# Eleven upper halves taken straight from the gate's PSUM bank, with a new order of work, in a fused attention and gated feed-forward kernel

## The chip, the cores and the metric

The kernel runs on one core of a Trainium2 chip. The metric is the device time in microseconds of one execution; a version's time is the median of its runs. The engines are named as in the profile: PE is TensorE, DVE VectorE, ACT ScalarE, POOL GpSimd, SP SyncE.

## The reference

Eight batches of blockwise causal attention (8 heads, 576 positions, head size 64, blocks of 64), and a gated feed-forward on the result:

```python
scores = scale * np.matmul(q, k.transpose(0, 1, 3, 2))
scores = np.where(block_i >= block_j, scores, -1000000000.0)
attn = softmax(scores)
x = matmul(attn, v)            # as (4608, 512)
gate = np.maximum(x @ w_gate, 0.0)
val = x @ w_val
out = gate * val @ w_out       # 512 -> 1536 -> 512
```

Inputs and output are float32; the kernel multiplies in bfloat16 and accumulates in float32.

## The kernel before

The 4608 tokens are worked in nine tiles of 512: tile j < 8 holds positions 0 to 511 of batch j, tile 8 the last 64 positions of all batches. Attention of batch j + 1 runs inside the feed-forward of tile j, so that TensorE has the one to do while other engines work on the other. Tiles 0 to 2 follow one long order and are not touched. Tiles 3 to 6 share one order written out by hand (ORDER_3_6); tiles 7 and 8 have their own. A function `program(j)` reads the order item by item and emits the instructions, so an item's place fixes its place in the queue of its engine. Which of an engine's buffers or banks an item gets is written down too (SLOTS, PAIR_BANK, OUT_BANK, AV_BANK), as is which of the elementwise items GpSimd does instead of VectorE (ON_POOL).

The hidden layer has twelve slices f of 128. Tiles 3 to 6 do f = 0, 1, 8 and 9 plainly (g, r, v, h: gate product, relu, value product, their product) and the other eight slices in four pairs (1, 2, 3, 5); tiles 7 and 8 do all twelve in six pairs. A pair computes gate and value for two slices at once with seven smaller products (Strassen's scheme with Winograd's sums). The products are the items p with a pair and a digit, as in 25; each is given twice, once for each of the two slices, and one item is two matmuls of 128x128 by 256 columns (L1363). They accumulate in three PSUM banks of the pair: w_ (products 1, 6, 5, 3), v_ (7, 4) and x_ (2). The items with a letter take the halves apart:

- a and u (ScalarE) copy w_ to SBUF, after product 1 and after product 6; w copies v_ after product 7 (L1385). c, d, e (VectorE) add what comes later in a bank to a copy (L1389).
- r (ScalarE) is relu of w_ once product 3 is in: the gate of the upper half of the tokens, written as bfloat16 to `gate_sb` (L1334). H multiplies it by the upper value half (L1401, VectorE or GpSimd).
- Without an r, H is a fused instruction on VectorE: max(w_, 0) times the value half, straight from the bank (L1405). L, the lower half, has always that form, from SBUF copies.

The copies lie in the buffers `ob` and, in tiles 7 and 8, `k_bf` and `q_bf`, which no attention needs any more. A pair's bank or buffer is given to its next user when all who read it are through.

The second weight product uses the same scheme once for the tile (M1 to M7, L1061, six parts of the hidden layer, c = 0 to 5, two to an item), with sums s of the hidden halves (L1020) and copies and adds oa, ou, ow, oy, oc, od, oe (L1106, L1100); S items issue the output's DMAs. X and Y are sums of token halves (L1171), U sums of weights for tiles 7 and 8 (L979). In attention A is the scores of two heads (L631), E their exponentials (L636, L643), C zeroes masked corners (L1516 on VectorE, L1519 on GpSimd), V multiplies by v and N normalises; T transposes the result into `xT` by DMA, d transposes q and k, and l and w load q, k and v of a later batch from GpSimd's queue (L509).

PSUM has eight banks: two `sc` of two each, one `one`, three `ffnp`.

Of the kernel before, what the change touches and what calls it, by code (L numbers as in the profile page):

```python
# [17 lines left out]
def kernel(  # L18
# [45 lines left out]
    ORDER_0 = """
# [36 lines left out]
        p0u p05*2 p21 p0w p1u p21 p04*2 p0d p0e p2a p15*2 p1w p1d p22 p03 p22 p03 p0r
        p31 p14*2 p13*2 p1r p26 p31 p0L p27 p26 p27 p2c p1e p1H Y5 p1L p37*2 p0H s0002
        s0202 s0102 p32*2 p2u p25 p3a p3c p36 p25 p36 p2w p24*2 p2d p2e p51*2 p3w p3u
        p35*2 p3d p23*2 p2L p34*2 p5a p56 p33*2 p2r p2H p3e p3L p52 p57 p56 p41 p57 p41
        p47 p3r p3H p52 p5c p42*2 p5u p55 p4a p4c p46*2 p47 p55 p5w p54 p5d p54 p5e M1
        s1002 s1202 s1102 p4w p4u p44*2 p4e p45 p53 p45 p4d p53 M1 p5r P p4L p5L p5H
        M2*2 M7 p43 M7 p43 p4r p4H s2002 s2202 s2302 M1*4 oa M2*4 M6*6 s2102 M7*4 ou
        M5*3 ow M5*3 od S2 oc M4*6 s1302 s0302 oe M3*4 S1 Y7 Y6 M3*2 oy S0
    """
    ORDER_8 = """  # L110
        p01 p31 p01 p0a p17 p11*2 p1a X4 p07 p17 p07 p0w p06 p12 p06 p0u p12 p1c p16*2
        p04 p05*2 p0d p21 p1u p15*2 p31 p1w p1d p14*2 p1e p3a p04 p1L p0e p21 p2a p03*2
        p0r p0H p13 p02 p13 p1r p02 p0c P p1H p36 p26*2 p2u p27*2 p2w p41 p32 p25 p32
        p41 p4a p25 s0002 p0L s0102 p2d p3c p37*2 p3w p36 p3u p24*2 p2e p23*2 p2r p2H
        p34*2 p3e p35 p47 p35 p3d p22*2 p47 p2c p4w p3L p2L p42 p51*2 p5a p42 p33*2 p3r
        p3H p4c p46*2 p56 p44*2 p4u p4e p4L p56 p5u p57*2 p5w p45*2 p4d p55*2 p5d p54*2
# [21 lines left out]
    }  # L138
    PAIR_BANK = {
        (3, 1): ('sc', 'sc', 'ffn'),  # L140
        (3, 2): ('one', 'sc', 'ffn'),
        (3, 3): ('ffn', 'sc', 'ffn'),
        (3, 5): ('ffn', 'one', 'ffn'),
        (4, 1): ('sc', 'sc', 'ffn'),
        (4, 2): ('one', 'sc', 'ffn'),
        (4, 3): ('ffn', 'sc', 'ffn'),
        (4, 5): ('ffn', 'one', 'ffn'),
        (5, 1): ('sc', 'sc', 'ffn'),
        (5, 2): ('one', 'sc', 'ffn'),
        (5, 3): ('ffn', 'sc', 'ffn'),  # L150
        (5, 5): ('ffn', 'one', 'ffn'),
        (6, 1): ('sc', 'sc', 'ffn'),
        (6, 2): ('one', 'sc', 'ffn'),
        (6, 3): ('ffn', 'sc', 'ffn'),
        (6, 5): ('ffn', 'one', 'ffn'),
        (7, 0): ('ffn', 'one', 'one'),
        (7, 1): ('sc', 'sc', 'sc'),
        (7, 2): ('ffn', 'ffn', 'ffn'),
        (7, 3): ('one', 'ffn', 'sc'),
        (7, 4): ('ffn', 'one', 'ffn'),  # L160
        (7, 5): ('sc', 'sc', 'ffn'),
        (8, 0): ('one', 'sc', 'ffn'),
        (8, 1): ('ffn', 'ffn', 'sc'),
        (8, 2): ('sc', 'one', 'sc'),
        (8, 3): ('ffn', 'ffn', 'ffn'),
        (8, 4): ('sc', 'ffn', 'one'),
        (8, 5): ('ffn', 'ffn', 'sc'),
    }
# [12 lines left out]
    OUT_BANK = {(2, 'v'): 'ffn', (2, 'w'): 'ffn', (2, 'x'): 'one', (3, 'v'): 'one', (3, 'w'): 'sc', (3, 'x'): 'ffn', (4, 'v'): 'one', (4, 'w'): 'sc', (4, 'x'): 'ffn', (5, 'v'): 'one', (5, 'w'): 'sc', (5, 'x'): 'ffn', (6, 'v'): 'one', (6, 'w'): 'sc', (6, 'x'): 'ffn', (7, 'v'): 'one', (7, 'w'): 'ffn', (7, 'x'): 'ffn', (8, 'v'): 'sc', (8, 'w'): 'ffn', (8, 'x'): 'one'}
# [857 lines left out]
    def seven_products(j, quads, sums):  # L1039
# [45 lines left out]
        def products(which):  # L1085
# [238 lines left out]
    def program(j):  # L1324
# [101 lines left out]
        def do(t):  # L1426
# [390 lines left out]
```

## Time and profile before

| | us |
|---|---|
| median of 3 runs | 344.81 (344.55 to 344.91) |
| profiled execution | 344.71 |
| its span, first to last instruction | 342.8 |
| one round of tiles 3 to 6 in it | 35.6 |

A line of a view names the engine, the source line, the operation, and output and inputs by the program's names. In a timeline the two numbers ahead are the start and the length in microseconds, xN counts like instructions that were put together, and the bracket is idle time ahead of them with what ended it. The length of a matmul covers its way through the array, so that neighbours overlap. Groups give the busy time, the mean of one in ns, and the idle time ahead of them.

### The profile page before, as it was taken

What the parts mean: (1) busy time and instruction counts of PE and PEld (TensorE: products, weight loads), DVE (VectorE), ACT (ScalarE), POOL (GpSimd) and SP (SyncE); (2) the same over time, 40 slices, a digit from 0 to 9 for tenths busy, and PEclk for the clock granted to TensorE, in tenths of its full rate; (3) what the DMA queues carried; (4) which work ended last, traced back from release to release, by engine and by line L of the source; (5) the groups of instructions that cost most, each with busy time, mean ns of one, the idle gap of its engine ahead of it and who ended that gap; (6) DMA issues with size and microseconds to landing.
All of it is one profiled execution on the core that took longest, in us unless ns stands there. A gap on an engine that the chain in (4) does not pass through costs nothing.

```text
span 342.8 us, 8917 instructions
## 1 busy us (share of the span) xinstructions
PE 332.7 (97%) x3477; PEld 233.8 (68%) x3518; DVE 233.1 (68%) x540; ACT 210.8 (61%) x344; POOL 216.7 (63%) x272
## 2 busy tenths in 40 slices
PE   8899999999999999999999999999999999999994
PEld 4544455545545558777877787777777788888883
DVE  4854445668637887389538972898279958966992
ACT  4942757588325882778558764876488727637731
POOL 2766566488695912787778967986514694750631
PEclk9999999999999999999999999999999999999998
DMA  8999999999998999799899989996510140002004
GB/s 242 294 351 371 368 230 238 240 163 155 187 197 137 144 158 137 165 143 121 111 165 120 130 116 153 128 137 118 138 33 2 33 122 12 2 31 94 33 0 122
DMA packets 155337, 50.06 MB, mean 146 GB/s; under 512 B 134496, under 2 KB 151648, under 8 KB 155296
## 3 DMA queue, kind: packets, MB, share of 16 engines
q0 software_dynamic: 70576, 9.12, 43.6%
q1 hardware_dynamic: 77536, 32.52, 43.0%
q10 hardware_dynamic: 7184, 7.87, 7.8%
q8 instruction: 27, 0.44, 0.5%
q14 instruction: 14, 0.11, 0.1%
HBM read 37.75 MB, written 9.44 MB: 138 GB/s over the span
## 4 chain that ended last, share of the span: by engine, by line
PE 88%; issue 4%; DVE 2%; ACT 2%; POOL 2%; POOLq 0%; DVEq 0%; ACTq 0%
PE ffnp L1179 16%; PE ffnp L1363 9%; PE ffnp L1339 8%; PE sc L1363 8%; PE sc L1061 6%; PE ffnp L1282 6%; PE ffnp L1061 6%; PE one L1363 5%; PE one L1061 4%; PE sc L631 3%; PE one L631 2%; PE one L779 2%; PE ffnp L779 2%; PE one L1179 2%; PE sc L779 1%
## 5 line engine op out<-in xcount | busy, mean ns | idle before, releaser
L636 ACT ACTIVATE attnT<-sc 128x1024 bf16<-128x1024 f32 x56 | 56.7, 1036 | 0.0
L1189 ACT ACTIVATE gate_sb<-ffnp 128x512 bf16<-128x512 f32 x35 | 20.6, 599 | 27.3 <-PE ffnp L1179 24.4
L1179 PE MATMUL ffnp<-xT,wg 128*128 128x512 bf16 x130 | 36.2, 379 | 0.6
L1061 PEld LDWEIGHTS <-stage 128*128 128x128 bf16 x336 | 32.0, 98 | 4.1 <-issue 0.2
L1363 PEld LDWEIGHTS <-stage 128*128 128x128 bf16 x288 | 27.3, 98 | 7.8
L779 PEld LDWEIGHTS <-attnT 128*128 128x128 bf16 x640 | 26.3, 98 | 7.7 <-DVE xnat L718 1.2
L1179 PE MATMUL ffnp<-xT,wv 128*128 128x512 bf16 x108 | 31.3, 380 | 0.2
L1199 DVE TENSOR_TENSOR hT<-gate_sb,ffnp 128x512 bf16<-128x512 bf16 x28 | 19.2, 684 | 14.9 <-PE ffnp L1179 12.0
L1389 DVE TENSOR_TENSOR ob<-ffnp,ob 128x512 f32<-128x512 f32 x29 | 19.8, 684 | 12.6 <-ACT ob L1385 12.6
L509 POOL DMA_DIRECT2D v_bf<-in_v_dram x30 | 24.3, 829 | 6.0 <-PE sc L793 3.1
L1061 PEld LDWEIGHTS <-hT 128*128 128x128 bf16 x252 | 24.2, 98 | 5.3 <-DVE hT L1405 1.1
L1363 PEld LDWEIGHTS <-wg 128*128 128x128 bf16 x224 | 21.9, 98 | 5.1
L1363 PEld LDWEIGHTS <-wv 128*128 128x128 bf16 x224 | 21.5, 98 | 5.3 <-ACT attnT L636 1.1
L1106 ACT COPY ob<-sc 128x512 f32<-128x512 f32 x13 | 7.6, 586 | 28.4 <-PE sc L1061 27.0
L1519 POOL MEMSET attnT<- 64x256 bf16 x34 | 10.2, 314 | 23.4 <-ACT attnT L636 16.0
L1282 PE MATMUL ffnp<-wo,hT 128*128 128x512 bf16 x91 | 23.1, 379 | 0.2
L1179 PEld LDWEIGHTS <-wg 128*128 128x128 bf16 x144 | 13.3, 98 | 13.8 <-issue 0.5
L1179 PEld LDWEIGHTS <-wv 128*128 128x128 bf16 x144 | 13.0, 98 | 14.3 <-issue 1.5
L1334 ACT ACTIVATE gate_sb<-ffnp 128x512 bf16<-128x512 f32 x30 | 17.6, 603 | 8.1 <-PE ffnp L1363 4.6
L509 POOL DMA_DIRECT2D q_bf<-in_q_dram x20 | 18.0, 908 | 5.0 <-DVE recip L752 4.0
L643 ACT ACTIVATE attnT<-one 128x512 bf16<-128x512 f32 (+1 forms) x28 | 15.0, 537 | 9.8 <-PE ffnp L631 8.4
L1020 POOL TENSOR_TENSOR stage<-hT,stage 128x512 bf16<-128x512 bf16 x15 | 17.4, 1167 | 4.2 <-DVE stage L1020 3.6
(228 smaller groups left out, 918.3 us busy)
## 6 DMA issues: line engine op xcount, KB each, us to landing
out_dram<-ob ACTq DMA_DIRECT2D x28, 256.0 KB, 3.4
stage<-in_moe_w_val_dram SPq DMA_DIRECT2D x6, 512.0 KB, 8.7
stage<-in_moe_w_gate_dram SPq DMA_DIRECT2D x6, 512.0 KB, 8.2
stage<-in_moe_w_out_dram SPq DMA_DIRECT2D x6, 512.0 KB, 10.5
q_bf<-in_q_dram POOLq DMA_DIRECT2D x20, 128.0 KB, 4.7
k_bf<-in_k_dram POOLq DMA_DIRECT2D x20, 128.0 KB, 5.5
v_bf<-in_v_dram POOLq DMA_DIRECT2D x20, 128.0 KB, 5.7
stage<-in_v_dram SPq DMA_DIRECT2D x19, 128.0 KB, 5.6
```

What stands on the lines that cost most here:

```text
L509: ins = nc.gpsimd.dma_start(dst, part_of)
L636: return lambda: nc.scalar.activation(at[:, :, lo : lo + 512], sc, AF.Exp, scale=scale)
L779: nc.tensor.matmul(av[:, p, :], at[:, col : col + 128], v_bf[b % 2][:, c, h, :], start=(p == 0), stop=(c == p), skip_group_check=True,)
L1061: nc.tensor.matmul(to, sums.of(c)[which][:, 128 * p : 128 * p + 128], right, start=first, stop=(c == 5), skip_group_check=True,)
L1179: nc.tensor.matmul(to, (wg, wv)[t][f // 4][:, c, 128 * (f % 4) : 128 * (f % 4) + 128], x[:, c], start=(c == 0), stop=(c == 3),)
L1189: nc.scalar.activation(gate_sb, gate, AF.Relu)
L1199: nc.vector.tensor_tensor(out=h, in0=gate_sb, in1=val, op=AX.mult)
L1282: nc.tensor.matmul(op, hT[f][:, 128 * s : 128 * (s + 1)], wo[f // 4][:, f % 4, n0:n1], start=(f == 0), stop=(f == 11),)
L1334: nc.scalar.activation(st[key], of, AF.Relu)
L1339: nc.tensor.matmul(to, (wg, wv)[t][f // 4][:, c, 128 * (f % 4) : 128 * (f % 4) + 128], x[:, c], start=(c == 0), stop=(c == 3),)
L1363: nc.tensor.matmul(st[key][:, 256 * k : 256 * k + 256], left[:, c, 128 * k : 128 * k + 128], right[:, c], start=new and (k, c) == (0, 0), ...
L1389: nc.vector.tensor_tensor(out=t, in0=st[n, of], in1=t, op=AX.add)
```

## The change

Pair 1 of tiles 3 to 6 (beside pair 2, which had none before), pairs 1, 3, 4 and 5 of tile 7 and pairs 1, 4 and 5 of tile 8 lose their r, and their H becomes the fused instruction on VectorE. The three orders, the banks and buffers and the split between VectorE and GpSimd are drawn anew. TensorE has the same 3518 matmuls as before; ScalarE has 11 relus fewer; VectorE has 11 fused products more (43), 7 two-operand operations fewer (353) and 4 memsets more; GpSimd has 4 two-operand operations and 4 memsets fewer. The core of the diff:

```diff
     ORDER_3_6 = """
-        l0 A0 E0t E0u g0*2 p12 w0 p12 X5 X7 E0s E0f X6 X4 K g0*2 g1*2 p11*2 p1a g1*2
-        p17*2 p16*2 C00 C01 p1c k V00 N00 P v1*2 p1u p15*2 p1w p1d p14 V01 N01 p14 p1e
-        p1L v1*2 r0 r1 p13*2 p1r v0*2 h1 A1 E1t v0*2 h0 p21*2 E1s p22*2 w1 p27*2 p2a
-        p26*2 E1u l1 w2 p31 p1H l2 l3 p2c p31 g8 U05 l4 p2w p24*2 w3 s0002 p2u p2e p2L
...
-        h8 p57 p51*2 p57 p52 E2s V10 N10 p5a p56*2 p5w d0 d1 T1 p5u s0202 p3H p52 p5c g9
...
-        M2*4 oc oy S0 w5 T3 U03
+        A0 X5 l0 w0 l1 E0t g1*2 E0f E0u E0s C01 X7 C00 g1 g0*3 p11*2 p1a X6 X4 g0 g1 K k
+        p12*2 p1c P p17*2 l2 p16*2 p1u V00 N00 v1*2 p15*2 p1w p1d v1*2 U05 l3 l4 l5 l6
+        l7 w1 r1 h1 r0 p14*2 p1e p27 V01 N01 U45 l8 p27 p2w w2 p1L v0*3 p21*2 v0 h0 p13
+        p22 p13 p1H s0102 p2a p22 p2c p24 p26*2 p31 p24 p31 p2u p2e p37 p25*2 p2d g8 p37
+        p3a p36 g8 p36 p2L p23*2 p3w p34 p3u p34 g8 p2H g8 r8 p35 p3e A1 E1t E1u E1f E1s
+        p35 p3d v8 p32*2 p3c w3 v8*3 h8 s0002 s0202 p33*2 p3r p51*2 p5a C10 p3L A2 E2u
...
+        g9*2 p54*2 p5u p5e g9 p55*2 p5d E2f C20 d0 T0 d1 d2 g9 r9 A3 E3f p53*2 p5r v9*4
...
+        M2 M7*2 ow M5*2 N30 N31 T3 M5*2 M4 M5*2 od S2 M2 M4*5 U46 oe S1 U47 U03 U07 w5
+        s0302 M3*6 oy S0 M2*4 oc U43
     ORDER_7 = """
...
-        s1002 s1202 s1102 p4w p4u p44*2 p4e p45 p53 p45 p4d p53 M1 p5r P p4L p5L p5H
-        M2*2 M7 p43 M7 p43 p4r p4H s2002 s2202 s2302 M1*4 oa M2*4 M6*6 s2102 M7*4 ou
...
+        p13 p1H p36*2 P p3u p24*2 p2e p37 p3w p25*2 p2d p51 s0002 s0202 p51 p5a p2L p35
+        p32*2 p3c p35 p23*2 p2r p2H p57 p34*2 p56 p57 p52 p5w p52 p3d p33*2 s0102 p3e
+        p5c p56 p5u p41*2 p4a p47*2 p3H s1002 p3L s1102 p54*2 p5e p42 p55*2 p5d p46*2
+        p42 p4c p4w p44*2 p4u p4e p45*2 p4d p4L p5L M1 p53 M2 M7 M2 p43*2 p4H M1 p53 p5H
+        s2002 s2202 M7 M1*4 M2*4 oa M6 s1202 M6*2 s2302 M6*3 ou s2102 M7*4 ow M5*6 M4*5
...
     ORDER_8 = """
...
-        p5e M2 p52 p43 p52 p5c p5L p53 p43 p4r p4H p53 p5r p5H M1*2 M2 M1*4 M2*4 s0202
-        s1002 s1202 oa s2002 s2202 M6*2 M7 s2102 M6*4 s1102 M7 s0302 s2302 M7*4 ou oca
-        Sa M5*5 ocb s1302 Sb ow M5 od M4 S2 M4*3 M3*3 oya Sya M4*2 oe S1 M3*3 oyb Syb
+        p44 p57*2 p5w p3H s1002 p4c p5c p44 p4e p56 s1102 p56 s1202 p5u p45*2 p4d p54*2
+        p5e M1 p55*2 p5d p5L p4L M1 M7*2 M2 p43*2 p4H p53*2 p5H s0202 s2002 s2202 M1 M2
+        M1*3 s2102 M2*4 oa M6*3 s0302 s1302 M6*3 M7*4 ou M5 ocb ow Sb M5*5 oca Sa od S2
+        M4*4 M3*2 s2302 M3 oya Sya M4*2 oe S1 M3*3 oyb Syb
...
     PAIR_BANK = {
         (3, 1): ('sc', 'sc', 'ffn'),
-        (3, 2): ('one', 'sc', 'ffn'),
-        (3, 3): ('ffn', 'sc', 'ffn'),
+        (3, 2): ('ffn', 'one', 'ffn'),
+        (3, 3): ('ffn', 'sc', 'one'),
         (3, 5): ('ffn', 'one', 'ffn'),
...
     ON_POOL = set(
         """
-        33H 35H 3C00 3C01 3C10 3C11 3C20 3C21 3C30 3C31 3X4 3X6 3X7 3s0102
-        3s0202 3s0302 3s1302 3s2202 3s2302 43H 45H 4C00 4C01 4C10 4C11 4C20 4C21
...
-        83H 8s0002 8s0102 8s1002 8s1202 U03 U06 U07 U46
+        33H 35H 3C00 3C01 3C10 3C11 3C20 3C30 3C31 3X4 3s0002 3s0102 3s0302
+        3s1002 3s1202 3s2202 3s2302 43H 45H 4C00 4C01 4C10 4C11 4C20 4C30 4C31
...
+        8s1102 8s1202 U03 U05 U06 U43 U45 U47
         """.split()
     )
-    OUT_BANK = {(2, 'v'): 'ffn', (2, 'w'): 'ffn', (2, 'x'): 'one', (3, 'v'): 'one', (3, 'w'): 'sc', (3, 'x'): 'ffn', ...
+    OUT_BANK = {(2, 'v'): 'ffn', (2, 'w'): 'ffn', (2, 'x'): 'one', (3, 'v'): 'one', (3, 'w'): 'ffn', (3, 'x'): 'ffn', ...
...
-    AV_BANK = {0: ('one', 'one'), 1: ('sc', 'sc'), 2: ('ffn', 'one'), 3: ('ffn', 'sc')}
+    AV_BANK = {0: ('one', 'ffn'), 1: ('ffn', 'ffn'), 2: ('sc', 'sc'), 3: ('ffn', 'sc')}
```

In ON_POOL and the banks the first digit is the tile; tiles 4, 5 and 6 have the same entries as tile 3. An s item has part of the hidden layer, sum, and range; 0102 is the sum of quarter 0 that M7 uses.

More of the change, by code (lines that the diff above doesn't have):

```diff
@@ L101 @@
[L101 to L105, printed above, removed]
-        s1002 s1202 s1102 p4w p4u p44*2 p4e p45 p53 p45 p4d p53 M1 p5r P p4L p5L p5H
@@ L107 @@
[L107 to L108 removed]
+        X5 X7 X6 p21 p01 p12 p11 p01 p0a p11 X4 p02 p12 p1a p1c p07*2 p02 p0w p06 p16
+        p06 p0c p16 p17 p04*2 p0u p0e p17 p05*2 p1u p15 p21 p0d p31 p22 p15 p0L p1w p1d
+        p2a p03*2 p0r p0H Y5 p26 p22 p14*2 p2c p31 p3a p27*2 p1e p1L p2w p26 p13 p2u p37
+        p13 p1H p36*2 P p3u p24*2 p2e p37 p3w p25*2 p2d p51 s0002 s0202 p51 p5a p2L p35
@@ L112 @@
[L112 to L116, printed above, removed]
-        p5e M2 p52 p43 p52 p5c p5L p53 p43 p4r p4H p53 p5r p5H M1*2 M2 M1*4 M2*4 s0202
@@ L118 @@
-        s1002 s1202 oa s2002 s2202 M6*2 M7 s2102 M6*4 s1102 M7 s0302 s2302 M7*4 ou oca
-        Sa M5*5 ocb s1302 Sb ow M5 od M4 S2 M4*3 M3*3 oya Sya M4*2 oe S1 M3*3 oyb Syb
+        p17 p01*2 p0a p11*2 p31 p1a p07*2 p17 p0w p12*2 p06*2 p1c p0u p16*2 X4 p04*2 p0e
+        p02 p05*2 p31 p0d p1w p14*2 p1u p15*2 p1e p1d p21*2 p03*2 p02 p3a p36 p13*2 p2a
+        p26*2 p0r p0H p37 p27 p2u p1L p0c p27 p2w p37 P p25*2 p32 p1H p0L s0102 s0002
+        p24 p32 p3w p2d p3c p24 p2e p36 p3u p34 p23*2 p2r p34 p3e p35*2 p3d p51 p41 p2H
@@ L140 @@
         (3, 1): ('sc', 'sc', 'ffn'),
-        (3, 2): ('one', 'sc', 'ffn'),
-        (3, 3): ('ffn', 'sc', 'ffn'),
+        (3, 2): ('ffn', 'one', 'ffn'),
+        (3, 3): ('ffn', 'sc', 'one'),
         (3, 5): ('ffn', 'one', 'ffn'),
         (4, 1): ('sc', 'sc', 'ffn'),
-        (4, 2): ('one', 'sc', 'ffn'),
-        (4, 3): ('ffn', 'sc', 'ffn'),
+        (4, 2): ('ffn', 'one', 'ffn'),
+        (4, 3): ('ffn', 'sc', 'one'),
         (4, 5): ('ffn', 'one', 'ffn'),
         (5, 1): ('sc', 'sc', 'ffn'),
-        (5, 2): ('one', 'sc', 'ffn'),
-        (5, 3): ('ffn', 'sc', 'ffn'),
+        (5, 2): ('ffn', 'one', 'ffn'),
+        (5, 3): ('ffn', 'sc', 'one'),
         (5, 5): ('ffn', 'one', 'ffn'),
         (6, 1): ('sc', 'sc', 'ffn'),
-        (6, 2): ('one', 'sc', 'ffn'),
-        (6, 3): ('ffn', 'sc', 'ffn'),
+        (6, 2): ('ffn', 'one', 'ffn'),
+        (6, 3): ('ffn', 'sc', 'one'),
         (6, 5): ('ffn', 'one', 'ffn'),
-        (7, 0): ('ffn', 'one', 'one'),
+        (7, 0): ('ffn', 'ffn', 'one'),
         (7, 1): ('sc', 'sc', 'sc'),
@@ L159 @@
         (7, 3): ('one', 'ffn', 'sc'),
-        (7, 4): ('ffn', 'one', 'ffn'),
-        (7, 5): ('sc', 'sc', 'ffn'),
-        (8, 0): ('one', 'sc', 'ffn'),
+        (7, 4): ('ffn', 'ffn', 'one'),
+        (7, 5): ('sc', 'ffn', 'ffn'),
+        (8, 0): ('one', 'sc', 'sc'),
         (8, 1): ('ffn', 'ffn', 'sc'),
-        (8, 2): ('sc', 'one', 'sc'),
+        (8, 2): ('sc', 'one', 'one'),
         (8, 3): ('ffn', 'ffn', 'ffn'),
```

42 lines of the change are left out of this document (19 added, 23 removed).

## The prediction

> **What bounds the kernel now.** I read the page first, then TensorE by stretches (one of tiles 3 to 6, then the end), then what TensorE waited for, then VectorE, ScalarE and GpSimd at those waits.
>
> ```profile
> span 342.8 us, 8917 instructions
> PE 332.7 (97%) x3477; PEld 233.8 (68%) x3518; DVE 233.1 (68%) x540; ACT 210.8 (61%) x344; POOL 216.7 (63%) x272
> ...
> PE 88%; issue 4%; DVE 2%; ACT 2%; POOL 2%; POOLq 0%; DVEq 0%; ACTq 0%
> ```
> ```profile
> core 0: us, PE busy (x) PEld busy (x) DVE busy (x) ACT busy (x) POOL busy (x), PEclk, DMA share, GB/s
> ...
> 199.68:235.29 35.61, 35.35 (x412) 27.43 (x416) 24.96 (x56) 24.55 (x41) 28.60 (x36) 1.00 1.31 131
> 235.29:270.91 35.62, 35.36 (x412) 27.45 (x416) 25.42 (x58) 24.57 (x41) 17.29 (x22) 1.00 0.28 61
> ```
>
> TensorE is the bound. In these two stretches, one round of the order each, it is busy 35.36 of 35.62 us at full clock, while VectorE has 25 us of work and ScalarE 24.6. An edit that only lightens those two engines is hidden there. What can still be gained lies where TensorE waits, and that is tiles 7 and 8:
>
> ```profile
> 301.13 0.27 PE L1061 MATMUL ffnp<-wo,hT 128*128 128x256 bf16 x1
> 301.64 1.81 PE L1061 MATMUL ffnp<-wo,hT 128*128 128x256 bf16 x15 [0.23 <-DVE hT L1405]
> ...
> 328.14 0.93 PE L1061 MATMUL ffnp<-wo,hT 128*128 128x256 bf16 x7
> 329.38 1.81 PE L1061 MATMUL ffnp<-wo,hT 128*128 128x256 bf16 x15 [0.31 <-DVE hT L1405]
> ...
> 333.69 1.47 PE L1061 MATMUL ffnp<-stage 128*128 128x256 bf16 x12
> 335.51 1.03 PE L1061 MATMUL sc<-stage,hT 128*128 128x256 bf16 x8 [0.35 <-ACT ob L1106]
> ```
>
> A row's length ends with its last matmul's 0.27 us, so seven matmuls in 0.93 us start (0.93 - 0.27) / 6 = 0.11 us apart; an item of the order (two matmuls) is 0.22 us. A row of n matmuls should be followed n x 0.11 us after its start. So TensorE lost 301.64 - 301.13 - 0.11 = 0.40 us in tile 7, 329.38 - 328.14 - 0.77 = 0.47 and 335.51 - 333.69 - 1.31 = 0.51 in tile 8: 1.38 us together. That is nearly all there is to win.
>
> **The change, part by part.**
>
> *Relu and product.* Eleven relus leave ScalarE (pair 1 in tiles 3 to 6; pairs 1, 3, 4, 5 in tile 7; 1, 4, 5 in tile 8; pair 2 of tiles 3 to 6 was already without one), and the eleven products become the fused form that reads the gate's bank.
>
> ```profile
> L1334 ACT ACTIVATE gate_sb<-ffnp 128x512 bf16<-128x512 f32 x30 | 17.6, 603 | 8.1 <-PE ffnp L1363 4.6 <-PE ffnp L1339 3.2
> L1405 DVE SCALAR_TENSOR_TENSOR hT<-one,ob 128x512 bf16<-128x512 f32 x4 | 2.8, 691 | 0.0
> L1401 DVE TENSOR_TENSOR hT<-gate_sb,ob 128x512 bf16<-128x512 bf16 x4 | 2.7, 686 | 0.0
> L1389 DVE TENSOR_TENSOR ob<-sc,ob 128x512 f32<-128x512 f32 x21 | 14.4, 684 | 5.7 <-PE sc L1363 5.1
> ```
>
> ScalarE loses 11 x 0.60 = 6.6 us; VectorE pays 0.69 for 0.69. A fused product from an `sc` or `ffnp` bank isn't in the trace; the rows for one from `one` and for an add from `sc` bound it by 0.68 and 0.69, so it costs nothing more. All this lies under TensorE: 0. What it can cost is the bank: it is free after VectorE's product instead of after the relu, and whoever is next in the bank waits.
>
> *Moves between VectorE and GpSimd.* Per tile 3 to 6, X6 and X7 and one corner go to VectorE and one more sum (s) to GpSimd.
>
> ```profile
> L1171 POOL TENSOR_TENSOR perm<-xT,perm 128x512 bf16<-128x512 bf16 x10 | 11.6, 1158 | 5.3 <-DVE perm L1171 4.8
> L1171 DVE TENSOR_TENSOR perm<-xT 128x512 bf16<-128x512 bf16 x5 | 2.2, 443 | 0.0
> L1020 DVE TENSOR_TENSOR stage<-hT 128x512 bf16<-128x512 bf16 x32 | 12.9, 418 | 0.6 <-POOL hT L1401 0.5
> L1516 DVE MEMSET attnT<- 64x128 uint32 x30 | 4.6, 165 | 3.3 <-ACT attnT L636 1.4 <-ACT attnT L595 1.0
> ```
>
> VectorE gets 2 x 0.44 + 0.17 - 0.42 = 0.63 us a tile, 25.6 of 35.6: covered. GpSimd gets lighter by about 2 x 1.16 + 0.31 - 1.17 = 1.5 us. In tile 8 one product (pair 3) comes back from GpSimd for 0.69 us of VectorE, and six instead of four weight sums of tile 6 go to GpSimd, which has 18 us free in that stretch. 0.
>
> *DMA.* SyncE's transposes change places (one xT ahead of kTm), and GpSimd issues nine loads in one run. The last xT transpose now stands 21 items, 21 x 0.22 = 4.6 us, ahead of the tile's end. I take 0; were it late, it would cost what the rivals below price for a late VectorE. None of the other transposes is consumed before the next tile.
>
> *End of tile 7.* M1's third item (c = 4, 5) needs the low products of pairs 4 and 5. Before, between pair 4's last 45 and that item stood 8 items (53, M1, M2, M2, M7, 43, M7, 43); now there are 10 (M1, 53, M2, M7, M2, 43, 43, M1, 53, M7). VectorE's pace is in the rows:
>
> ```profile
> 299.70 0.68 DVE L1389 TENSOR_TENSOR q_bf<-ffnp,q_bf 128x512 f32<-128x512 f32 x1
> 300.30 1.28 DVE L1405 SCALAR_TENSOR_TENSOR hT<-ob,k_bf 128x512 bf16<-128x512 f32 x2
> ...
> 328.63 0.69 DVE L1405 SCALAR_TENSOR_TENSOR hT<-ob,k_bf 128x512 bf16<-128x512 f32 x1
> ```
>
> It starts one every 0.60 us. Pair 4's u-add (e) is still running when the last 45 starts (call it 0), so d begins at 0.64, the two low products at 1.24 and 1.84, and the second ends at 2.52; TensorE arrives at 0.11 + 10 x 0.22 = 2.31. The lack is 0.2 us, and with some 0.05 us as the same sum misses before (0.35 for the measured 0.40) 0.25 us. Change: 0.25 - 0.40 = -0.15.
>
> *End of tile 8.* The same item now stands 8 items (M1, M7, M7, M2, 43, 43, 53, 53) behind the last 55, TensorE arriving at 1.85 us. VectorE has pair 5's e until 0.43, then d, low product 5, low product 4, started at 0.43, 1.03, 1.63 and ended at 2.31. Lack 0.46 to 0.52; the same sum gave 0.34 before where 0.47 was lost, so 0.60 us. Change: +0.13. The direct products of pairs 4 and 5 stand behind these in VectorE's queue, and the bank one of them holds is wanted 0.36 us too early; that is under the 0.60.
>
> *The third wait* is ScalarE's:
>
> ```profile
> 332.80 0.59 ACT L1106 COPY ob<-ffnp 128x512 f32<-128x512 f32 x1 [1.86 <-PE ffnp L1061]
> 333.36 1.47 ACTq L906 DMA_DIRECT2D out_dram<-ob  x2
> 334.87 0.59 ACT L1106 COPY ob<-sc 128x512 f32<-128x512 f32 x1 [1.49 <-DVE stage L1020]
> ```
>
> The copy `ow` stands behind two output issues (Sa, Sb) that take 1.47 us of ScalarE's queue; M4 needs the bank that `ow` empties. In the new order `ow` stands ahead of both, five M5 items (1.09 us) ahead of M4; copy and hand-over take 0.6 + 0.1. The wait goes: -0.51. The issues then lie under M5 and M4.
>
> *GpSimd against VectorE.* One row of the trace speaks against this order:
>
> ```profile
> 154.87 0.69 DVE L1405 SCALAR_TENSOR_TENSOR hT<-one,ob 128x512 bf16<-128x512 f32 x1
> ...
> 156.79 1.34 DVE L1405 SCALAR_TENSOR_TENSOR hT<-ob,ob 128x512 bf16<-128x512 f32 x1
> ```
> ```profile
> 155.20 1.15 POOL L1020 TENSOR_TENSOR stage<-stage,hT 128x512 bf16<-128x512 bf16 x1
> ...
> 156.42 1.17 POOL L1401 TENSOR_TENSOR hT<-gate_sb,ob 128x512 bf16<-128x512 bf16 x1
> ```
> ```profile
> L1405 DVE SCALAR_TENSOR_TENSOR hT<-ob,ob 128x512 bf16<-128x512 f32 x16 | 13.6, 851 | 0.6
> ```
>
> A low product with both operands in SBUF, begun 0.37 us after GpSimd's product, took 1.34 us where it usually takes 0.69; the group's 13.6 us are twelve of 0.69 and four of 1.34, one a round. The product with a PSUM operand took 0.69 beside GpSimd's sum. So a VectorE operation of two SBUF operands waits until GpSimd's is done. The Trainium skill, "SBUF — State Buffer", section "Who interferes with whom", says the same: VectorE with two SBUF inputs and GpSimd reading SBUF exclude each other, the first to issue keeps the pair, and one SBUF input does not contend. By that rule the eleven direct products become immune, a gain wherever one would have been caught; by the trace pair 1's four products in the rounds took 0.686 us on average (L1401 above), so none was caught there, and the sum is no other.
>
> In tile 7 the new order has GpSimd make two sums back to back (s0002, s0202) once pair 1's high product is done, the second 1.15 us after that product's end; VectorE has two adds to do (1.2 us, and some 0.1 of waiting for TensorE) and reaches pair 2's low product 1.3 us after it, 0.15 us after the second sum began. It then waits some 0.9 us. Behind it in the queue are pair 3's c, d, e and the next adds. Counted in items, the bank of the add d (`one`) is wanted 0.6 us after its usual end, and that of the add three places on 0.21 us, with 0.27 us of idle time between: late by 0.3, then 0.9 - 0.27 - 0.21 = 0.4. I take +0.42; its bounds are 0 (VectorE is first) and 0.6 (1.15 - 0.27 - 0.21, and a little).
>
> Sum: -0.15 + 0.42 + 0.13 - 0.51 = -0.11 us, against the profiled execution's own 344.71. That is 344.6, and the median of the runs shown (344.81) is 0.10 above that execution: **344.7 us**.
>
> **Rivals.**
>
> *VectorE wins in tile 7.* No collision: -0.53, 344.3. For it: only 0.15 us decides. Against: the four collisions of the present rounds (1.34 us each) show that such a place repeats closely.
>
> *The collision in the round of tiles 3 to 5 (slower).* After its memsets and X4, GpSimd issues nine loads and then s0102:
>
> ```profile
> 175.91 2.38 POOL L1171 TENSOR_TENSOR perm<-xT,perm 128x512 bf16<-128x512 bf16 x2 [1.92 <-DVE perm L1171]
> 178.35 0.55 POOL L1519 MEMSET attnT<- 64x256 bf16 x2
> ...
> 181.50 1.78 POOL L509 DMA_DIRECT2D q_bf<-in_q_dram  x2
> 183.24 0.72 POOL L509 DMA_DIRECT2D q_bt<-in_q_dram  x1
> 183.92 0.92 POOL L509 DMA_DIRECT2D v_bf<-in_v_dram  x1
> 184.79 1.80 POOL L509 DMA_DIRECT2D k_bf<-in_k_dram  x2
> ```
>
> Starts lie 0.87 us apart (0.68 behind q_bt). Memsets 0.6, X4 1.2, eight of the issues and q_bt's 7.7: s0102 starts 9.5 us after the first memset. From the end of the scores A0 TensorE has 10.8 us of items up to pair 2's last 25 (14 of pair 1, 12 of pair 2, 3 of pair 3 and 16 plain products at 0.22 us each, and two heads' products with v, 0.9 in all); add and hand-over make 0.9 more, and the memset starts some 2.4 us behind A0, when four exponentials are through. So VectorE reaches pair 2's low product 9.3 us after the memset, ahead by about 0.25 us. If it is not, the low product waits 1.1 us, and with it ScalarE's copy into the `ob` that it frees, whose bank is wanted 0.28 us after that copy's usual end: 0.8 us in each of tiles 4 and 5, +1.7, 346.4. It decides from 0.25 us of delay on VectorE or haste on GpSimd. Against it: in tile 6, without loads, the sums come earlier and catch the product for 0.35 us only, 0.07 of it felt.
>
> *A bank held too long in the round.* A direct product or an add that is 0.2 us later than I place it, in a round where the smallest distance I find between an add and the next matmul in its bank is about nothing (an add of pair 3's u ahead of the plain products of f = 8, 9), costs that four times: +0.8 to 1.2, 345.7. For it: TensorE waits nowhere in the present round, so every change of order can only lose there.
>
> *The change doesn't do what it says in the round*, since three of four upper halves lie as before: there 0, and all comes from the ends, which is my forecast too. A better end than I find (lack in tile 8 only 0.3) gives 343.9.
>
> **How the numbers follow.** Forecast 0.42; no collision 0.17 (344.3); collision in tiles 4 and 5 0.2 (346.4); bank in the round 0.13 (345.7); better ends 0.08 (343.9). 0.2% is 0.69 us, about what this kernel's measurement can tell; faster means under 344.12. Faster: all of the better ends, two fifths of the case without collision, and a twentieth of the forecast, 0.08 + 0.07 + 0.03 = 0.18. Slower: the two slower cases and a little of the forecast, 0.35. Same: 0.47. The range is 343.9 to 346.5; the likeliest case's own is 344.2 to 345.2.
>
> **What would show it.** Right: rounds of 35.6 us with no wait on TensorE; in tile 7 a low product of about 1.5 us beside a GpSimd sum and a TensorE wait of 0.4 us some 2 us later; at the end of tile 8 a wait of 0.6 us for a low product, and none for `ow`. Wrong: rounds over 35.8 us, a low product over 1.3 us in tiles 4 and 5, or ScalarE's copies waiting for VectorE there.

## The result, and the profile after

| | median, us | single times | against the kernel before |
|---|---|---|---|
| before, beside the first runs | 344.68 | 344.5 to 345.5 | |
| changed, first runs (6) | 346.67 | 345.1 to 348.3 but for one | 1.0052 (95%: 1.0030 to 1.0074) |
| changed, run again (12) | 346.99 | 345.0 to 349.6 | 1.0057 (1.0032 to 1.0082) |

The change makes the kernel 0.5% slower, 1.9 us, where 344.7 (343.9 to 346.5) was forecast. It also makes it scatter: three in four runs of the kernel before lie within half a microsecond, those of the changed one over more than three. One of the first six executions took 353.77 us and is left out of the ratio; the other five have a median of 346.44. That one was profiled and was held up by some 7 us ahead of tile 3, where both programs are the same, so the profile read here is one of the second series (347.99 us, its span 346.2). The changed kernel's source is a line shorter, so that L1405 of the kernel before is L1404 in it. First its page:

```profile
span 346.2 us, 8912 instructions
PE 334.1 (96%) x3481; PEld 235.0 (68%) x3518; DVE 234.8 (68%) x548; ACT 204.0 (59%) x333; POOL 210.8 (61%) x264
...
PE 86%; issue 4%; DVE 3%; ACT 3%; DMA 2%; POOL 1%; POOLq 0%; ACTq 0%
```

ScalarE has lost 6.8 us of work and the end hasn't come nearer; VectorE's and ScalarE's share of the chain went from 2% to 3% each, and the 2% of DMA are new. Then TensorE by stretches from the scores A0 of one tile to those of the next (tiles 3, 4, 5, then 6 to the end; columns: the stretch, its length, and the busy time of each engine), of the kernel before and of the changed one:

```profile
139.00:174.71 35.71, 35.45 (x413) 27.36 (x418) 23.93 (x54) 24.98 (x41) 29.77 (x37) 1.00 1.21 135
174.71:210.32 35.61, 35.35 (x412) 27.43 (x416) 24.95 (x56) 24.56 (x40) 28.59 (x36) 1.00 1.30 130
210.32:245.94 35.62, 35.36 (x412) 27.44 (x417) 24.95 (x56) 24.56 (x40) 26.83 (x34) 1.00 1.18 139
245.94:342.80 96.86, 91.36 (x916) 76.41 (x920) 72.02 (x139) 55.69 (x96) 45.98 (x46) 0.99 0.16 46
```
```profile
139.24:175.18 35.94, 35.69 (x415) 27.67 (x418) 24.10 (x56) 24.38 (x40) 27.45 (x34) 1.00 1.31 130
175.18:212.38 37.20, 35.74 (x414) 27.56 (x418) 26.03 (x58) 23.90 (x39) 27.22 (x34) 1.00 1.36 129
212.38:249.59 37.21, 35.57 (x415) 27.70 (x418) 26.33 (x58) 23.80 (x39) 24.61 (x31) 1.00 1.21 130
249.59:346.20 96.61, 91.59 (x917) 76.83 (x920) 71.71 (x141) 50.88 (x88) 45.46 (x45) 0.99 0.16 47
```

Nothing is lost at the end: the last stretch is 0.25 us shorter, though tile 6, a round of the new order, lies in it. The loss is in the rounds: 0.23 us in tile 3, and 1.59 us each in tiles 4 and 5. What happened in tile 5, in the timeline of the changed kernel (a load's issue on GpSimd, pair 2's low product on VectorE, GpSimd's sum s0102, ScalarE's copy into the buffer that the product frees, and TensorE):

```profile
224.38 0.95 POOL L508 DMA_DIRECT2D v_bf<-in_v_dram  x1
...
224.78 2.28 DVE L1404 SCALAR_TENSOR_TENSOR hT<-ob,ob 128x512 bf16<-128x512 f32 x1
...
225.27 1.24 POOL L1019 TENSOR_TENSOR stage<-hT 128x512 bf16<-128x512 bf16 x1
...
227.16 0.58 ACT L1384 COPY ob<-ffnp 128x512 f32<-128x512 f32 x1 [1.96 <-DVE hT L1404]
...
227.79 0.38 PE L1362 MATMUL ffnp<-perm,stage 128*128 128x256 bf16 x2 [1.48 <-ACT ob L1384]
```

The product of two SBUF operands starts 0.49 us ahead of the sum and still ends 0.55 us behind the sum's end, so it waited for that sum: 2.28 us instead of 0.68. ScalarE's copy waits for it, and TensorE 1.48 us for the copy. In tile 4 the same product took 1.99 us and TensorE waited 1.19 us. (Another part of tile 4's loss is no collision: at 180.93 us a copy of ScalarE's had waited 0.60 us until an output transfer out of its `ob` buffer had landed, 7.09 us after its issue, and TensorE's next matmuls were 0.28 us late. That transfer is the DMA in the chain.) In tile 3 it won, and the sum was the one that waited (1.43 us instead of 1.16):

```profile
151.35 0.94 POOL L508 DMA_DIRECT2D v_bf<-in_v_dram  x1
...
151.76 0.90 DVE L1404 SCALAR_TENSOR_TENSOR hT<-ob,ob 128x512 bf16<-128x512 f32 x1
...
152.24 1.43 POOL L1019 TENSOR_TENSOR stage<-hT 128x512 bf16<-128x512 bf16 x1
```

Tiles 3 and 5 begin alike to 0.01 us, 0.41 and 0.40 us after the start of a load's issue, and end 1.4 us apart. The first profiled execution bears this out: its rounds take 35.92, 35.83 and 37.21 us, its products 0.89, 0.90 and 2.28 us. From A0 of tile 3 to TensorE's last matmul it needs 200.95 us with one loss, the execution above 202.33 us with two, the kernel before 199.20 us. So the number of losses changes from one execution to the next. Single times of 345.0 to 349.6 us in the second series fit none to three losses, but only these two executions have a trace.

The rest of the loss is much the same in every round. TensorE and VectorE around the heads' products and the scores A3 in tile 3:

```profile
159.37 0.69 DVE L1388 TENSOR_TENSOR ob<-ffnp,ob 128x512 f32<-128x512 f32 x1 [0.17 <-PE ffnp L1362]
...
159.95 0.19 PE L792 MATMUL ffnp<-v_bf,attnL 128*128 128x65 bf16 x1
...
160.11 0.38 PE L1338 MATMUL ffnp<-xT,wg 128*128 128x512 bf16 x1
...
161.25 0.69 DVE L1388 TENSOR_TENSOR ob<-one,ob 128x512 f32<-128x512 f32 x1 [0.29 <-PE one L1362]
...
161.63 0.38 PE L1338 MATMUL ffnp<-xT,wg 128*128 128x512 bf16 x1
...
161.99 0.27 PE L630 MATMUL one<-qTm,kTm 64*128 64x256 bf16 x1
```

The adds c and e of pair 5 end at 160.06 and 161.94, and 0.05 us behind each stands the matmul that takes its bank. A matmul of 512 columns is followed by the next 0.21 us on, so A3 is 161.99 - 161.63 - 0.21 = 0.15 us late; the first is late by 0.13 us against other places with the same neighbours. The kernel before has one such place in each round, its A1, which starts 0.31 us behind a matmul of 512 columns and is 0.10 us late. That leaves 0.18 us a round.

The end of tile 8 on TensorE (the first two rows around the start of the last M1 items, the next two around that of M4, whose bank the copy ow empties):

```profile
332.26 0.60 PE L1362 MATMUL ffnp<-xTt,stage 128*128 128x256 bf16 x4
333.27 2.14 PE L1060 MATMUL ffnp<-wo,hT 128*128 128x256 bf16 x18 [0.41 <-DVE hT L1404]
...
337.43 1.47 PE L1060 MATMUL ffnp<-stage 128*128 128x256 bf16 x12
338.74 1.04 PE L1060 MATMUL one<-stage,hT 128*128 128x256 bf16 x8
```

333.27 - 332.26 - 0.44 = 0.57 us of wait for the low product, and none at M4: it starts 1.31 us behind the row ahead of it, which is that row's twelve matmuls at 0.11 us. So ow is no longer waited for.

### The profile page after: what moved, and what is told of

Read it like the earlier page. It is cut to its first block, busy times and chain, and to the rows that moved or that the text cites. A ratio compares the mean times of both kernels' runs of the same rounds, so it can differ in the third digit from the quotient of the medians.

```text
span 352.0 us, 8949 instructions
## 1 busy us (share of the span) xinstructions
PE 338.4 (96%) x3518; PEld 235.7 (67%) x3518; DVE 235.4 (67%) x548; ACT 204.0 (58%) x333; POOL 211.4 (60%) x264
## 4 chain that ended last, share of the span: by engine, by line
PE 87%; issue 4%; DVE 3%; ACT 2%; DMA 2%; POOL 1%; POOLq 0%; DVEq 0%; ACTq 0%
PE ffnp L1178 14%; PE ffnp L1362 12%; PE ffnp L1060 12%; PE ffnp L1338 8%; PE sc L1362 7%; PE ffnp L1281 6%; PE one L1362 4%; PE one L1060 4%; PE sc L630 3%; PE ffnp L778 3%; PE one L630 2%; DMA qTt<-q_bt 2%; ACT attnT L594 2%; PE one L1178 2%; PE one L778 1%
## 5 line engine op out<-in xcount | busy, mean ns | idle before, releaser
L1105 ACT COPY ob<-ffnp 128x512 f32<-128x512 f32 x22 | 12.9, 586 | 48.8 <-PE ffnp L1060 41.9
L1518 POOL MEMSET attnT<- 64x256 bf16 x30 | 8.7, 306 | 50.7 <-ACT attnT L635 50.0
L1178 PE MATMUL ffnp<-xT,wg 128*128 128x512 bf16 x140 | 38.6, 386 | 0.0
L1188 ACT ACTIVATE gate_sb<-ffnp 128x512 bf16<-128x512 f32 x35 | 20.5, 599 | 29.7 <-PE ffnp L1178 29.5
L1178 PE MATMUL ffnp<-xT,wv 128*128 128x512 bf16 x112 | 32.5, 385 | 0.5 <-DVE hT L1198 0.5
L1019 POOL TENSOR_TENSOR stage<-hT 128x512 bf16<-128x512 bf16 x20 | 24.0, 1209 | 7.0 <-DVE hT L1404 4.2
L1388 DVE TENSOR_TENSOR ob<-ffnp,ob 128x512 f32<-128x512 f32 x27 | 18.6, 687 | 12.7 <-ACT ob L1384 8.4
L1384 ACT COPY ob<-ffnp 128x512 f32<-128x512 f32 x30 | 18.1, 603 | 12.8 <-PE ffnp L1362 9.4
L1099 DVE TENSOR_TENSOR ob<-ffnp,ob 128x512 f32<-128x512 f32 (+1 forms) x15 | 9.7, 655 | 22.7 <-PE ffnp L1060 21.6
```

The lines of the kernel that those rows point to most:

```text
L1019: (eng or nc.vector).tensor_tensor(out=of(part), in0=a, in1=b, op=op)
L1178: nc.tensor.matmul(to, (wg, wv)[t][f // 4][:, c, 128 * (f % 4) : 128 * (f % 4) + 128], x[:, c], start=(c == 0), stop=(c == 3),)
L1188: nc.scalar.activation(gate_sb, gate, AF.Relu)
L1388: nc.vector.tensor_tensor(out=t, in0=st[n, of], in1=t, op=AX.add)
```

## The experiments

Theory A: what is lost is the collision of pair 2's low product with GpSimd, in none to three tiles an execution, and a small steady wait at pair 5's banks; the ends gain. Its rivals: only the steady waits (B); the transposes and loads, or what comes ahead of tile 3 (C); the ends gain nothing (D); the direct product itself costs (E) or gains (F).

**The changed kernel again** (a_again).

> The changed kernel once more. Theory A (pair 2's low product and GpSimd's s0102 reach SBUF nearly together; where the product loses, it takes 2.3 us instead of 0.9 and TensorE loses 1.4 us, in none, one, two or three of tiles 3 to 5 as chance has it): single times lie in steps of about 1.4 us above 345.2, median 346.0 to 346.7, and the profile shows as many low products over 2 us as its time is steps above 345.2. Theory B (a steady cost: each round loses 0.27 us at two banks that pair 5 holds, and the collision was an accident of one execution): times within 0.4 us of 345.3, no low product over 1.3 us. Theory C (transposes and loads are late in the changed order): TensorE's waits in tiles 3 to 8 end with a DMA.

Measured 346.99 (345.04 to 349.56), 0.3 us above A's range, with the two long products shown above in an execution of 347.99. A and not B. No wait of TensorE in tiles 3 to 8 ended with a DMA by itself; C's part in this execution is the 0.28 us in tile 4, behind a copy that waited for an output transfer.

**The sum moved in GpSimd's queue** (b_sum_first, c_sum_one_earlier, d_sum_later; each against the changed kernel):

```diff
-  ... l7 w1 r1 ... U45 l8 p27 p2w w2 p1L ... p1H s0102 p2a
+  ... l7 r1 ... U45 p27 p2w p1L ... p1H s0102 w1 l8 w2 p2a        (sum first)
+  ... l7 w1 r1 ... U45 l8 p27 p2w p1L ... p1H s0102 w2 p2a        (one earlier)
+  ... l7 w1 r1 ... U45 l8 p27 p2w w2 p1L ... p1H l9 s0102 p2a     (later; l9 from behind N10)
```

> Three load issues (w1, l8, w2) stand behind s0102 instead of ahead of it in tiles 3 to 5, so that the sum runs 2.5 us earlier and is done 0.8 us before the low product starts. Theory A: no low product over 1.0 us, no sum lengthened beside one, scatter of single times under 0.6 us, median 345.0 to 345.4, the remaining +0.5 against the kernel before being the bank waits of 0.27 us a round less the gain at the ends. Theory B: as the changed kernel. Theory C: slower than the changed kernel, since three loads are issued 1.2 us later.

> One load issue (w2) stands behind s0102 instead of ahead of it: the sum starts about 0.4 us ahead of the low product and is in possession when the product comes. Theory A: in each of tiles 3 to 5 the low product waits for the sum, 0.8 us, and takes 1.4 to 1.6 us every time; TensorE loses 0.3 to 0.8 us a tile; steady times of 346.1 to 347.5. Theory B and C: 346.0 to 346.7 as the changed kernel, or 345.3.

> One more load issue (l9, 0.67 us) stands ahead of s0102, so that the low product is always first. Theory A: low products of 0.7 to 0.9 us in tiles 3 to 5, the sum is the one that waits (1.4 us), steady times of 345.0 to 345.4, as with the sum first. Theory B: 345.3 also for the changed kernel. Theory C: as the changed kernel or slower.

One earlier: 346.68, single times from 346.46 to 347.15 only. The sum now holds the path to SBUF (whatever it is that keeps the two from working at once) when the product comes, and every one of the three tiles is alike (1.40, 1.42, 1.42 us; GpSimd's sum, the product and TensorE in tile 3):

```profile
151.16 1.23 POOL L1019 TENSOR_TENSOR stage<-hT 128x512 bf16<-128x512 bf16 x1
...
151.54 1.40 DVE L1404 SCALAR_TENSOR_TENSOR hT<-ob,ob 128x512 bf16<-128x512 f32 x1
...
153.67 0.38 PE L1362 MATMUL ffnp<-perm,stage 128*128 128x256 bf16 x2 [0.60 <-ACT ob L1384]
```

A collision that always happens costs 0.6 us of TensorE a tile and takes the scatter away; that is theory A's mechanism, made steady. Later: 346.33, and here A's expectation failed. In two of three tiles the product took 1.4 us with no sum near. Tile 4 of that kernel:

```profile
187.44 0.94 POOL L508 DMA_DIRECT2D v_bf<-in_v_dram  x1
...
187.84 1.42 DVE L1404 SCALAR_TENSOR_TENSOR hT<-ob,ob 128x512 bf16<-128x512 f32 x1
...
188.30 0.71 POOL L508 DMA_DIRECT2D k_bt<-in_k_dram  x1
...
188.95 1.31 POOL L1019 TENSOR_TENSOR stage<-hT 128x512 bf16<-128x512 bf16 x1
```

It begins 0.40 us into a load's issue and, at its usual 0.68 us, can't have begun to work before 188.58, ahead of the sum by 0.37 us and behind the issue that it met. Nothing else of GpSimd's stands beside it, so it looks as if the issue of a load can keep the product out by itself; tile 5, alike to 0.01 us, got away with 0.80 us. Sum first: products of 0.68 us and no collision in the profiled execution (345.98, of which 1.08 us was lost ahead of tile 3), as A says, but a median of 346.47 and single times up to 347.7, where A said 345.0 to 345.4. Run again (k_sum_first_again):

> The kernel with the sum first once more, for a second profile: its single times lay between 345.5 and 347.7 where theory A gave 345.0. Theory A': in some executions pair 2's low product comes in the second half of a load's issue (w1 or l8) and takes 1.2 to 1.4 us: an excess over 345.0 in steps of about 0.5 us, each with such a product in the trace. Rival C: the excess stands ahead of tile 3, rounds of 35.8 to 35.9 us.

346.50 again, ten of twelve from 345.9 to 347.2, while the profiled execution of 344.77 shows rounds of 35.8 us and products of 0.68 us. What the others lost isn't in a trace, so this run decides nothing between A' and C by itself.

**Taking the loads out of the way** (f_v_loads_last, i_five_loads_last).

```diff
-  A0 X5 l0 w0 l1 ... l7 w1 r1 ... U45 l8 p27 p2w w2 p1L ... p1H s0102 ... p3c w3 v8*3 h8 s0002 s0202
+  A0 X5 l0 l1 ... l7 l8 r1 ... p1H s0102 ... p3c v8*3 h8 s0002 w0 w1 w2 w3 s0202       (f)
+  A0 X5 l0 l1 ... l7 r1 ... p1H s0102 ... p3c v8*3 h8 s0002 l8 w0 w1 w2 w3 s0202       (i)
```

> The changed kernel with the four v loads w0 to w3 of the rounds behind s0002, so that GpSimd does s0102 and s0002 as soon as pair 1's high product is done, and issues no load while pair 2's low product runs. Theory A, as it now stands (the second half of a load's issue keeps VectorE's two SBUF operands out as well as a sum does): low products of 0.7 to 0.9 us, no wait of TensorE for them, 344.9 to 345.2 and single times within 0.5 us of each other. Rival C (what scatters is the part ahead of tile 3, with its transposes): 345.5 to 347.5, spread as with the sum first.

> The changed kernel with five load issues of the rounds (l8 and w0 to w3) behind s0002, so that the two sums start 0.8 us earlier than with four behind, as they do in tile 6, where no loads are. Theory A: low products of 0.8 us in tiles 3 to 5 as in tile 6, no wait of TensorE over 0.25 us there; rounds of 35.8 us, median 344.9 to 345.3, single times within 0.6 us of each other. Rival C (scatter from ahead of tile 3): 345.5 to 347.5 with rounds of 35.8 us.

The first missed its aim and A's range: four k loads still stood ahead of the sums, the second sum began 0.1 us ahead of the product, and the product took 1.63 or 1.64 us in each of the three tiles: 347.41. With one load more behind, 344.88 (344.64 to 345.34; before 344.78 beside it, ratio 1.0002, 0.9993 to 1.0010): loss and scatter are gone. The sums and the product in tile 3 of that kernel:

```profile
149.69 2.27 POOL L1019 TENSOR_TENSOR stage<-hT 128x512 bf16<-128x512 bf16 x2
...
151.70 0.82 DVE L1404 SCALAR_TENSOR_TENSOR hT<-ob,ob 128x512 bf16<-128x512 f32 x1
...
151.91 0.92 POOL L508 DMA_DIRECT2D k_bf<-in_k_dram  x1
```

The direct products, the banks, the order on TensorE and the ends are those of the changed kernel; only load issues have moved, and with them the place of GpSimd's two sums. So all but some 0.1 us of the loss in the times lies in when GpSimd does its work beside that one product.

**At which moment of an issue?** The kernel with the sum first, with one, two or three memsets of 0.3 us on GpSimd (zeros over zeros, tiles 3 to 5) between s0102 and the loads (l, m, n).

```diff
-  p1H s0102 w1 l8 w2 p2a
+  p1H s0102 Z w1 l8 w2 p2a            (Z*2, Z*3)
+  elif k == "Z":
+      if j < 6:
+          nc.gpsimd.memset(zeros[0:64, 0:256], 0.0)
```

> The kernel with the sum first, and in tiles 3 to 5 one memset of 0.3 us (zeros written over zeros) on GpSimd right behind s0102, so that the load issues start 0.3 us later and pair 2's low product starts about 0.55 us into one of them instead of at its start. Theory A' (the second half of a load's issue keeps out a VectorE operation with two SBUF operands, with no sum near): low products of 1.0 to 1.4 us in all of tiles 3 to 5, in the profiled execution too; rounds 0.3 to 0.6 us longer than 35.8. If only GpSimd's sums keep it out: low products of 0.7 us, rounds of 35.8 us, 345.0.

> As the kernel with one memset behind s0102, with two: pair 2's low product now starts some 0.4 us into the issue of w1. In the traces so far it started at 0.41 us into an issue with 0.8 to 2.3 us of length, and at 0.0 and 0.65 with 0.68. Theory A'' (an issue asks for the SBUF path at about 0.4 us and a product that comes just then may lose it, to the rest of the issue alone): low products of 0.8 to 1.4 us though no sum is near, rounds up to 0.6 us longer. If only a sum can keep it out: 0.7 us in all tiles.

> With three memsets the low product starts some 0.1 us into the issue of w1. Theory A'': 0.68 us in all of tiles 3 to 5 in the profiled execution, and single times nearer to 345.0 than with one (345.6) or two memsets. If any issue under way keeps it out, 0.9 us or more.

Medians 345.57, 344.84 and 344.77, after 346.5 with none. With one memset the expectation failed in the profiled execution: the product, 0.65 us into one issue and ahead of the next by 0.26 us, took 0.68 us in all three tiles:

```profile
151.01 0.92 POOL L508 DMA_DIRECT2D v_bf<-in_v_dram  x1
...
151.66 0.68 DVE L1404 SCALAR_TENSOR_TENSOR hT<-ob,ob 128x512 bf16<-128x512 f32 x1
...
151.92 0.88 POOL L508 DMA_DIRECT2D k_bf<-in_k_dram  x1
```

With two the product came 0.04 us behind an issue's start or ahead of it, so the place aimed at (0.4 us into one) was not tried again. With three it starts beside the last memset and has 0.3 us of start on the issue (tile 4):

```profile
186.20 1.02 POOL L1458 MEMSET zeros<- 64x256 bf16 x3
...
187.10 0.68 DVE L1404 SCALAR_TENSOR_TENSOR hT<-ob,ob 128x512 bf16<-128x512 f32 x1
...
187.42 0.92 POOL L508 DMA_DIRECT2D v_bf<-in_v_dram  x1 [0.20 <-issue]
```

The medians fall as the issues move back; but for the memsets only what stands behind them in GpSimd's queue moves. That argues for load issues close to the product as what costs time in most executions of the kernel with the sum first, but no trace shows it. Late loads aren't it: the five-loads kernel issues them later still. Output transfers that hold an `ob` buffer, as in tile 4 above, weren't ruled out: the longest of the rounds took 5.4 and 5.9 us in the two profiles of the sum first, 5.3 to 5.6 us with memsets and 4.1 us with five loads behind. Which moment of an issue is the dangerous one beyond the 0.4 us seen stays open too.

Part of the scatter is common to all: an execution of the kernel with two memsets (346.01) lost 1.3 us ahead of tile 3, where every kernel here has the same program:

```profile
64.68 0.41 PE L681 MATMUL sc<-qTt,kTm 64*128 64x64 bf16 x16 [1.31 <-DVE hT L1198]
```

**Old rounds with new ends** (e_old_rounds_new_ends): orders, banks, buffers and engine split of tiles 3 to 6 from the kernel before, of tiles 7 and 8 from the changed one.

> Tiles 3 to 6 as in the kernel before, tiles 7 and 8 as in the changed kernel. Theory A (the loss is made in the rounds: 0.18 us a round at pair 5's banks and up to three collisions; the new ends are worth 0.44 us): 344.3 to 344.5, spread of single times as before, no low product over 1.4 us in the rounds, no wait for ow. Rival D (the ends gain nothing by themselves, the profile's 0.44 us belongs to the new rounds' last tile): 344.7 to 344.9. Rival C (prefix and transposes): as the changed kernel, 346 to 347.

344.63, ratio 0.9990 (0.9979 to 1.0002). TensorE's last matmul starts 198.61 us after A0 of tile 3, 0.59 us earlier than before (199.20). In the profiled execution the last output took 0.6 us longer to land and gave that back (0.4 us in that of the next experiment), and the median is 0.2 us below the kernel before, beside it. The ends gain on TensorE: not D, though the times show less than half of it. The rounds of this kernel are 35.62 us long: the loss is in the rounds.

**The end of tile 8** (j_ends_m2_first; on e).

```diff
-  p53*2 p5H s0202 s2002 s2202 M1 M2 M1*3
+  p53*2 p5H s0202 s2002 s2202 M2 M1 M1*3
```

> Rounds of the kernel before, ends of the changed one, and in tile 8 the last two items ahead of M1*3 exchanged (M2 M1 for M1 M2), so that one more item lies between pair 5's low product and the M1 item that needs it. Theory A (the 0.58 us there is the wait for that product): 0.36 us of wait, 0.22 us off the run with old rounds and new ends, 344.2 to 344.4; if the wait is for something else, 344.5 to 344.7.

The wait behind it is 330.05 - 329.47 - 0.22 = 0.36 us, as expected:

```profile
329.47 0.38 PE L1061 MATMUL ffnp<-wo,hT 128*128 128x256 bf16 x2
330.05 1.16 PE L1061 MATMUL ffnp<-wo,hT 128*128 128x256 bf16 x9 [0.19 <-DVE hT L1405]
```

344.49, ratio 0.9988 (0.9980 to 0.9997): the fastest version here, by a little, and it has the old rounds. But of the 0.22 us only 0.09 arrive at TensorE's last matmul (91.58 us behind A0 of tile 6 against 91.67 without the exchange), since two later waits grow by 0.13, and 344.2 to 344.4 was missed. The same exchange on top of the five loads (o_loads_last_m2_first):

> The changed kernel with both repairs: the five load issues behind s0002, and M2 M1 for M1 M2 at the end of tile 8. If the two are independent: 344.88 - 0.22 = 344.66, spread under 0.7 us; the new rounds then still stand 0.2 to 0.3 us behind the old rounds with the same ends (344.49).

345.14 (344.68 to 346.08). The wait in tile 8 is 0.36 us there too, but the last matmul comes only 0.06 us earlier (91.92 against 91.98 us behind A0 of tile 6), and 0.43 us was lost ahead of tile 3 in the profiled execution. That the two add up is not shown.

**Form and order apart** (g_relus_back: the new order with the eleven r items put back ahead of their H; h_direct_alone: the old order with them taken out, and p1H of the rounds right behind p13*2).

> The changed kernel's order, banks and buffers, with the eleven relus back on ScalarE and products of two bfloat16 operands in SBUF. Theory A (the order's loads and sums are the cost, not the form of the product): collisions as in the changed kernel, 345.5 to 347.5. Theory E (the direct product is the cost, since it holds the bank until VectorE comes): 344.2 to 344.8. By the trace of the changed kernel pair 1's product would start 0.25 us into a load's issue; if that keeps it out, it is 0.6 us late and 0.7 us long, and the time is 0.5 to 1 us above the changed kernel's.

> The kernel before with the same eleven products taken from the bank, its order otherwise kept, but for pair 1's high product in the rounds, which stands right behind product 3 (ahead of h1, h0 and A1, whose bank it holds). Theory A: A1 waits 0.1 to 0.5 us a round for the bank, the ends lose 0.2 to 0.6 us at pairs 4 and 5: 345.3 to 347.0; so the direct product without a new order is no gain. Theory F (the relus on ScalarE are worth time by themselves): 343.8 to 344.6.

353.30 and 349.96, both far outside every theory's range. (Of the two operands of a product with a relu only the gate is bfloat16; the value half in `ob` is float32.) With the relus back the low product collides in each of tiles 3 to 5, as theory A has it (1.39 to 1.40 us); collisions of that length cost 0.6 us a tile with the sum one earlier, so they are the smaller part of the 8.5 us here. In the new order pair 1's relu goes ahead of the copy p2a on ScalarE, and TensorE waits for that copy (ScalarE, then TensorE):

```profile
149.68 0.60 ACT L1334 ACTIVATE gate_sb<-sc 128x512 bf16<-128x512 f32 x1 [1.37 <-PE sc L1363]
...
150.17 0.58 ACT L1385 COPY ob<-ffnp 128x512 f32<-128x512 f32 x1
...
150.81 0.38 PE L1363 MATMUL ffnp<-perm,stage 128*128 128x256 bf16 x2 [0.72 <-ACT ob L1385]
```

In the old order the scores A1 wait for the bank that the direct product reads behind VectorE's queue (VectorE, then TensorE):

```profile
148.87 0.68 DVE L1405 SCALAR_TENSOR_TENSOR hT<-sc,ob 128x512 bf16<-128x512 f32 x1
...
149.60 0.39 PE L631 MATMUL sc<-qTm,kTm 64*128 64x384 bf16 x4 [0.73 <-DVE hT L1405]
```

Each order is fitted to its form of the product; neither run prices the form alone, and E and F stay undecided beyond that.

## Why the prediction was wrong

The step that failed is the term for the rounds of tiles 3 to 6, which the prediction put at 0 ("there 0, and all comes from the ends"), with the collision in the rounds a rival at 0.2 and a late bank another at 0.13, as if one excluded the other. Both came: each round costs some 0.17 us more, and each collision that the product loses 1.2 to 1.5 us of TensorE.

- *The collision's place was right, its odds and price weren't.* VectorE was to be ahead of s0102 "by about 0.25 us"; it is ahead by 0.19 to 0.49 us and loses in two of the three tiles shown, and in one of three in the first profiled execution. Being ahead by its recorded start was not enough, as the prediction took it to be. I counted from the sum's start alone and left out that GpSimd is in the issue of a load when the product comes. The price was to be 1.1 us of wait and 0.8 us of stall a tile; it is 1.3 to 1.6 us and 1.2 to 1.5 us.
- *The banks.* The steady loss is 0.17 us a round (35.78 against 35.61 us in tile 4 of the kernel with three memsets, which has no collision), made at the adds c and e of pair 5 (0.28 us, less the 0.10 that the old round loses at its A1), not at pair 3's where the smallest distance was found. So the old round was not quite without waits, as the prediction had it.
- *Tile 7, the term of +0.42.* It didn't come. GpSimd's hand-over took longer than I placed it and VectorE won by nothing: the second sum is recorded at 296.35, the product at 296.36, and the sum took 1.71 us while the product took its 0.68:

```profile
295.12 1.16 POOL L1019 TENSOR_TENSOR stage<-hT 128x512 bf16<-128x512 bf16 x1 [1.46 <-DVE hT L1404]
...
296.35 1.71 POOL L1019 TENSOR_TENSOR stage<-stage,hT 128x512 bf16<-128x512 bf16 x1
296.36 0.68 DVE L1404 SCALAR_TENSOR_TENSOR hT<-ob,k_bf 128x512 bf16<-128x512 f32 x1
```

- *The ends.* Tile 8: 0.57 us for the forecast 0.60. The wait for ow is gone, as forecast. In tile 7 the wait at M1 is gone altogether (0.25 was forecast), and TensorE loses 0.25 us at pair 4's products 5 and 3 instead. Together -0.59 us for the rival's -0.53.
- *The form.* Direct products from `sc`, `ffnp` and `one` took 0.68 to 0.69 us each (677 to 692 ns), as bounded; the moves between VectorE and GpSimd are covered.

So without the collision the sum is -0.59 + 4 x 0.17 = +0.1 us. From A0 of tile 3 to TensorE's last matmul the traces without a collision give 199.28 us (three memsets) and 199.43 (five loads), where tile 6 loses 0.15 more, against 199.20 before. The medians are 344.88 with five loads against 344.78 of the kernel before beside it, 344.84 and 344.77 with two and three memsets against 344.82, and 345.14 against 344.82 with five loads and the exchange at the end of tile 8. Less its collision the change is worth about nothing, as forecast, but that is luck: the 0.42 us of tile 7 that didn't come and the rounds' 0.7 us that weren't counted nearly cancel. Most of the measured 1.9 us is the collision.

## What to carry to other kernels

Where a VectorE operation with two SBUF operands comes less than half a microsecond ahead of GpSimd's next sum, and in the middle of a load's issue, don't count it as safe: here it lost in three of the six rounds traced. Price the whole of what stands in GpSimd's queue there, load issues too, and count it for every tile that repeats it. Moving load issues behind the sums cost nothing here and was worth about 2 us. A slack of "about nothing" in a round is a small loss in each round, not a rival.

## What the runs showed of the hardware

The recorded start of an instruction doesn't tell which engine has the path. The product lost though recorded 0.49 us ahead of the sum (2.28 us), and another won though recorded 0.01 us behind one (0.68 us). And a VectorE operation of two SBUF operands was held up with nothing but load issues on GpSimd beside it: 1.40 and 1.42 us at 0.41 and 0.40 us into an issue, the next sum 1.1 us away (0.80 us in the third tile, at 0.40 us too). At 0.01 us (sum first) and 0.65 us (one memset) into an issue the same product took 0.68 us; how long the dangerous part is, no run here shows. The Trainium skill, "SBUF — State Buffer", section "Who interferes with whom", infers for a tensor_tensor of two SBUF inputs that it stays clear of descriptor generation, since the one needs the path's read side and the other its write side. If the same holds for the product here, which has two SBUF inputs as well, the 1.42 us speak against it.
